# Decoding the gated product's weights through PSUM, and two banks instead of four for its first group

## The chip, the cores and the metric

The kernel runs on one core of a Trainium2 chip. Its engines are PE (matrix products, with PEld loading weights beside it), DVE (vector), ACT (scalar), POOL (GpSimd) and SP (which issues DMAs). Each has a queue of its own, worked off in order, and waits for the others by semaphores. The metric is the device time of one execution in microseconds, as a median of several runs.

## What is computed

Three layers in one program: an attention with pooled queries, a mixture of experts with a capacity, and a gated product. Only the last one is touched here:

```python
def _moe2_setup():
    n_tokens, d_model, d_ff = (1152, 512, 1536)
    ...
def _moe2_ref(x, w_a, w_b, w_out) -> np.ndarray:
    a = x @ w_a
    b = x @ w_b
    return (a * b @ w_out).astype(np.float32)
```

The three weights come as float64. The kernel turns each of their 64-bit words into a 32-bit one with integer operations (the decode), splits that into a high and a low part, and makes each product from three: high x high, low x high, high x low.

## The kernel before

**The gated product.** The 1536 inner columns are cut into 12 blocks f. For each f there are two upward products, s1(f, 0) with w_a and s1(f, 1) with w_b, and a downward one, s2(f) with w_out. Each is a unit of twelve matmuls on PE. The tokens go in groups: 512 wide, then 320 wide. PE's order is written out in `cons`: s1(0, 0), s1(0, 1), s1(1, 0), s1(1, 1), s2(0), s1(2, 0), s1(2, 1), s2(1), and so on, 36 units; unit k uses weight k. For f from 1 on, s1(f, 1) is unit 3f and s2(f) unit 3f + 4. Weights are decoded during the first group only; the second finds them ready.

**Around one f.** ACT copies s1(f, 0) out of PSUM (`copy_a`, L1428), DVE multiplies s1(f, 1) with that (`times`, L1431), ACT makes the high part gh (L1435), POOL the low part gl (L1438). s2(f) needs gh for its first eight matmuls and gl for its last four. There are two gh buffers and one gl.

**The decode.** Nine of the 36 words are ready when the first group starts. For each of the other 27, ACT writes the absolute value of the upper half into one of three SBUF ring buffers, parts of the tile y (`absval`, L1200); DVE makes four steps: step 0 (L1180) clamps it in place, step 1 (L1183) shifts and masks it in place, step 2 (L1186) adds the sign bit out of the upper half, step 3 (L1189) adds bits of the lower half and writes the word back where it was fetched. ACT then makes the word's high part (L1375), POOL its low part (L1378). `tick` puts the steps of two neighbouring words in turn on DVE's queue: step 0 of word k + 1, step 2 of k, step 1 of k + 1, step 3 of k.

**What sets the order.** `first` and `group` give each piece of work a due time on a made-up clock, sort by it and issue it so; the order on every engine is fixed by that, whatever the chip's times are. Slots for fetched words are released by `tick` and by the splits; the next fetch into a slot waits for them on SP's queue.

**PSUM.** Of the eight banks, four hold the sums of the downward product (`oa0` to `oa3`) and four, under the name `ab`, take the upward products in turn.

Of the kernel before, what the change touches and what calls it, by code (L numbers as in the profile page):

```python
# [9 lines left out]
F32 = mybir.dt.float32  # L10
# [305 lines left out]
def fused_kernel(tc, q, k, v, w_gate, w1, w2, cap_in, w_a, w_b, w_out, out):  # L316
    nc = tc.nc
# [15 lines left out]
    def as_f32(bits):  # L333
        return struct.unpack("<f", struct.pack("<I", bits))[0]

    def pool(name, **kw):
        return tc.tile_pool(name=name, bufs=1, **kw)
# [272 lines left out]
    def scatter(dst, idx, src, group):  # L610
        nc.gpsimd.memset(spacer, 0.0)
        inst = nc.gpsimd.indirect_dma_start(out=dst, out_offset=bass.IndirectOffsetOnAxis(ap=idx, axis=0),  # L612
                                            in_=src, in_offset=None)
        ins = inst.ins if hasattr(inst, "ins") else inst
        for o in groups.setdefault(group, []):
            tc.declare_no_dep(ins, o, reason="scattered rows are distinct")
        groups[group].append(ins)
# [214 lines left out]
    class Banks:  # L832
        n, wide = 0, None
# [335 lines left out]
    def halves(a):  # L1169
        return a.rearrange("p (h n) -> p h n", h=2)  # L1170

    def words(k):
        return halves(raw64[k].rearrange("p n w -> p (n w)")).rearrange("p h (n w) -> p h n w", w=2)

    def decode_step(hw, lw, c, step, out=None):
        ci = c.bitcast(I32)
        if step < 0:
            nc.vector.tensor_scalar(out=ci, in0=hw, scalar1=0x7FFFFFFF, scalar2=None, op0=ALU.bitwise_and)
        elif step == 0:
            nc.vector.tensor_scalar(out=c, in0=c, scalar1=as_f32(0x38000000), scalar2=as_f32(0x47EFFFFF),  # L1180
                                    op0=ALU.max, op1=ALU.min)
        elif step == 1:
            nc.vector.tensor_scalar(out=ci, in0=ci, scalar1=3, scalar2=0x3FFFFFF8,  # L1183
                                    op0=ALU.logical_shift_left, op1=ALU.bitwise_and)
        elif step == 2:
            nc.vector.scalar_tensor_tensor(out=ci, in0=hw, scalar=-0x40000000, in1=ci,  # L1186
                                           op0=ALU.bitwise_and, op1=ALU.bitwise_or)
        else:
            nc.vector.scalar_tensor_tensor(out=ci if out is None else out, in0=lw, scalar=29, in1=ci,  # L1189
                                           op0=ALU.logical_shift_right, op1=ALU.bitwise_or)  # L1190

    def decode_words(hw, lw, c):
        for step in range(-1, 4):
            decode_step(hw, lw, c, step)

    def decode(k, c, step, out=None):
        decode_step(words(k)[:, :, :, 1], words(k)[:, :, :, 0], c, step, out)

    def absval(k, c):
        nc.scalar.activation(c, words(k)[:, :, :, 1].bitcast(F32), AF.Abs)  # L1200
# [144 lines left out]
    pf = mid.enter_context(pool("psf", space=PSUM))  # L1345
# [9 lines left out]
    def wt(f, i, p, c=None):  # L1355
        t = (HI, LO)[p][cons.index((f, i))]
        return t if c is None else t[:, c * 128:c * 128 + 128]
# [10 lines left out]
            nc.vector.tensor_tensor(out=yl[:, c, 0:w], in0=src, in1=yh[:, c, 0:w].bitcast(F32), op=ALU.subtract)  # L1368

    ring = [y[:, 0:2, N:N + 256], y[:, 2:4, N:N + 256], y[:, 2:4, 0:256]]  # L1370

    def split_hi(k):
        if k >= KX:
            own(fp if k < KB else yp, k)
        nc.scalar.activation(halves(HI[k]), packed[k], AF.Copy)  # L1375
# [4 lines left out]
    def tick(k):  # L1380
        for d, i in ((1, 0), (0, 2), (1, 1), (0, 3)):
            if PK <= k + d < NK:
                n, at = k + d, k - 1 if k in SECOND else k
                out = words(at)[:, :, :, 1 if at < k else 0] if i == 3 else None
                decode(n, ring[n % 3], i, out)
                if i == 3:
                    packed[k] = out.bitcast(F32)
        if PK <= k + 2 < NK:
            absval(k + 2, ring[(k + 2) % 3])
# [5 lines left out]
    def first(plan):  # L1395
        DV, PO = T["dv"], T["po"]
        for k in range(PK - 2, NK):
            t = T["t0"] + (k - PK) * DV
            plan.append((t, lambda k=k: tick(k)))
            if ("t", k) in FREED:  # L1400
                plan.append((t, lambda k=FREED["t", k]: fetch(k)))
        ready = {}
        for k in range(NL, NK):
            t = PO * (k - NL) - T["p0"]
            if k >= PK:
                t = max(t, T["t0"] + (k - PK) * DV + .1)
            ready[k] = t + .5
            plan += [(t, lambda k=k: split_hi(k)), (t + .4, lambda k=k: split_lo(k))]
            if ("s", k) in FREED:
                plan.append((t + .5, lambda k=FREED["s", k]: fetch(k)))  # L1410
        return ready

    def group(o, w, nxt=None):
        by_token = o == 0
        oa = [pf.tile([128, 512], F32, name=f"oa{c}", bufs=1) for c in range(KD)]
        ab, gs = {}, {}
        asb, gg = y[:, 0, o:o + w], y[:, 1, o:o + w]

        def s1(f, i):
            p = ab[f, i] = pf.tile([128, 512], F32, name="ab", bufs=4)  # L1420
            seq = [(wt(f, i, 0, c), yh[:, c, 0:w]) for c in range(KD)]
            seq += [(wt(f, i, 1, c), yh[:, c, 0:w]) for c in range(KD)]
            seq += [(wt(f, i, 0, c), yl[:, c, 0:w]) for c in range(KD)]
            for n, (a, x) in enumerate(seq):
                nc.tensor.matmul(p[:, 0:w], a, x, start=(n == 0), stop=(n == len(seq) - 1))  # L1425
# [36 lines left out]
        for n, (f, i) in enumerate(cons):  # L1462
            now = max(now, ready.get(n, 0.0) + .05)
            if i == 2:
                now = max(now, t[f] + T["gl"] + .01)
                plan.append((now, lambda f=f: s2(f)))
            else:
                plan.append((now, lambda f=f, i=i: s1(f, i)))
                if i == 0:
                    plan.append((now + unit + .02, lambda f=f: copy_a(f)))  # L1470
                else:
                    t[f] = now + unit + .02
                    for d, fn in ((T["gg"], times), (T["gh"], g_hi), (T["gl"], g_lo)):
                        plan.append((t[f] + d, lambda f=f, fn=fn: fn(f)))
            now += unit
            if n == NK - 2 and nxt is not None:
                plan.append((now, lambda: split_y(nxt, min(W1, N - nxt))))
# [19 lines left out]
        def rows_out(t, last):  # L1497
            n = min(128, w - t)
            at = ids[min(o, W0)][:n, (o - min(o, W0) + t) // 128]
            rows = slots[RAW + t // 128][:n, 0:DM]  # L1500
            for g in range(0, KD, 2 if last else KD):
                cs = range(g, g + 2 if last else KD)
                p = pf.tile([128, 512], F32, name="ab", bufs=4)
                for c in cs:
                    nc.tensor.transpose(p[:n, (c - g) * 128:(c - g) * 128 + 128], ot[:, c, t:t + n], ident)
                r = rows[:, g * 128:(g + len(cs)) * 128]
                if last and g == 0:
                    nc.vector.tensor_scalar(out=r, in0=p[:n, 0:256], scalar1=at[:, 0:1], scalar2=None, op0=ALU.mult)
                else:
                    nc.scalar.activation(r, p[:n, 0:len(cs) * 128], AF.Copy, scale=at[:, 0:1])  # L1510
            scatter(out, at[:, 1:2].bitcast(I32), rows, "out")
        for t in range(0, w, 128):
            rows_out(t, nxt is None)
# [38 lines left out]
```

## Time and profile before

| | us |
|---|---|
| median of 3 runs (637.14 to 637.78) | 637.65 |
| the profiled execution | 637.94 |
| its span, first to last instruction | 636.2 |
| PE busy in the span | 575.6 (90%) |
| DVE busy | 392.9 (62%) |
| POOL busy | 364.6 (57%) |
| ACT busy | 307.4 (48%) |

The gated product takes the span's last 195 us: its first group runs from 441.5 to 559.8, the second one from there to about 624. The shares over the span mix stages with different limits, so the section with the rows reads single stretches. In a row of the timeline stand the start, the duration, the engine, the line, the operation, what it writes and reads, the shape, the count, and in brackets how long the engine stood idle before it and for whom. Instructions of one engine overlap by a little: the next may start before the duration of the last is over. Matmuls of a row marked x8 are eight in one.

### The profile page before, as it was taken

How to read it: one execution, taken by the hardware profiler on the slowest of the kernel's cores; microseconds unless marked ns; L12 is line 12 of the kernel's file. 1: busy time of each engine (PE TensorE's matmuls, PEld its weight loads, DVE VectorE, ACT ScalarE, POOL GpSimd, SP SyncE). 2: the span in 40 equal slices, each digit the busy share in tenths (PEclk: the TensorE clock that was granted, in tenths of full speed). 3: DMA queues.
4: the chain of work that ended last, by engine and by line, in shares of the span. 5: the costliest groups of instructions: out<-in, count | busy, mean ns of one | idle time of the engine just before them, and what ended most of it. 6: DMA issues, size and time to landing. Idle time of an engine off the chain costs nothing. (4 is left out here: it accounts for less than half of the span.)

```text
span 636.2 us, 10735 instructions
## 1 busy us (share of the span) xinstructions
PE 575.6 (90%) x3956; PEld 437.7 (69%) x3956; DVE 392.9 (62%) x702; ACT 307.4 (48%) x686; POOL 364.6 (57%) x291
## 2 busy tenths in 40 slices
PE   4798999999999999999997976998988798899993
PEld 3565666666666666656796974985776576699992
DVE  8667575756568595513568783746999999420001
ACT  6855566575656556455753422624344444321111
POOL 3966575757668896884538835751654565441112
PEclk9799999999999999999998888999999999999997
DMA  7902544224252624964397996999953020010001
GB/s 167 219 1 44 125 165 107 65 45 106 44 124 44 173 55 146 309 170 145 117 316 232 312 312 137 330 367 310 339 159 103 0 67 1 1 66 1 1 1 46
DMA packets 75998, 87.06 MB, mean 137 GB/s; under 512 B 24002, under 2 KB 57410, under 8 KB 75938
## 3 DMA queue, kind: packets, MB, share of 16 engines
q1 hardware_dynamic: 74258, 82.22, 44.8%
q0 software_dynamic: 1680, 4.07, 1.9%
q8 instruction: 33, 0.54, 0.3%
q14 instruction: 27, 0.22, 0.1%
HBM read 73.16 MB, written 6.43 MB: 125 GB/s over the span
## 5 line engine op out<-in xcount | busy, mean ns | idle before, releaser
L220 POOL TENSOR_TENSOR acc<-acc,E 128x1152 f32<-128x1152 f32 x52 | 137.5, 2644 | 52.3 <-ACT E L194 51.8
L161 DVE TENSOR_REDUCE MX<-tr 128x1 f32<-128x384 f32 x202 | 108.4, 554 | 74.8 <-PE tr L159 71.8
L194 ACT ACTIVATE E<-sc 128x288 f32<-128x288 f32 x288 | 108.1, 409 | 94.3 <-PE sc L193 89.7
L200 PE MATMUL pv<-E,vt 128*64 128x288 f32 x576 | 101.6, 431 | 0.0
L1425 PE MATMUL ab<-yh,w 128*128 128x512 f32 (+1 forms) x336 | 69.7, 349 | 0.0
L1425 PEld LDWEIGHTS ab<-yh,w 128*128 128x128 f32 x336 | 57.0, 188 | 6.8
L1438 POOL TENSOR_TENSOR gl<-y,gh 128x512 fp32r<-128x512 f32 (+1 forms) x24 | 27.9, 1164 | 54.3 <-PE oa L1455 47.2
L1378 POOL TENSOR_TENSOR w<-w,w 128x512 fp32r<-128x512 f32 x22 | 31.5, 1435 | 45.8 <-ACT w L1375 30.7
L1431 DVE TENSOR_TENSOR y<-ab,y 128x512 f32<-128x512 f32 (+1 forms) x24 | 14.1, 586 | 62.4 <-PE ab L1425 57.1
L200 PEld LDWEIGHTS pv<-E,vt 128*64 128x64 f32 x576 | 28.7, 134 | 26.0 <-issue 24.9
L1425 PE MATMUL ab<-yl,w 128*128 128x512 f32 (+1 forms) x168 | 38.2, 349 | 0.0
L220 POOL TENSOR_TENSOR acc<-E 128x1152 f32<-128x1152 f32 x8 | 21.2, 2651 | 29.3 <-ACT E L194 29.0
L192 PE MATMUL sc<-ra,even 128*128 128x288 f32 x108 | 34.8, 329 | 1.0 <-ACT E L194 1.0
L1375 ACT ACTIVATE w<-w 128x512 fp32r<-128x512 f32 x22 | 14.6, 675 | 38.4 <-DVE w L1189 38.4
L1425 PEld LDWEIGHTS ab<-yl,w 128*128 128x128 f32 x168 | 28.9, 188 | 3.3
L1183 DVE TENSOR_SCALAR y<-y 128x512 int32<-128x512 int32 x27 | 30.1, 1114 | 0.0
L192 PEld LDWEIGHTS sc<-ra,even 128*128 128x128 f32 x108 | 20.7, 192 | 13.0 <-ACT E L194 8.5
L1445 PE MATMUL oa<-w,gh 128*128 128x512 f32 x96 | 24.2, 394 | 4.3 <-ACT gh L1435 4.3
L159 PE MATMUL tr<-even,ra 128*128 128x384 f32 x74 | 27.1, 390 | 0.9 <-DVE MX L161 0.9
L1428 ACT ACTIVATE y<-ab 128x512 f32<-128x512 f32 (+1 forms) x24 | 12.2, 510 | 29.2 <-PE ab L1425 29.2
L1435 ACT ACTIVATE gh<-y 128x512 fp32r<-128x512 f32 (+1 forms) x24 | 13.2, 548 | 26.4 <-DVE y L1431 26.4
L1445 PEld LDWEIGHTS oa<-w,gh 128*128 128x128 f32 x96 | 17.7, 188 | 9.5 <-ACT gh L1435 6.0
(405 smaller groups left out, 1485.0 us busy)
## 6 DMA issues: line engine op xcount, KB each, us to landing
rw<-in_moe_w_dram SPq DMA_DIRECT2D x21, 512.0 KB, 9.9
s_even<-in_moe_w_dram SPq DMA_DIRECT2D x12, 512.0 KB, 9.7
s_ra<-in_moe_w_dram SPq DMA_DIRECT2D x12, 512.0 KB
w<-in_moe_w_dram SPq DMA_DIRECT2D x12, 512.0 KB, 9.0
vt<-in_v_dram SPq DMA_DIRECT2D x8, 576.0 KB
s_qs<-in_moe_w_dram SPq DMA_DIRECT2D x9, 512.0 KB, 7.8
w<-in_moe_w_a_dram SPq DMA_DIRECT2D x9, 512.0 KB, 9.4
qs<-in_q_dram SPq DMA_DIRECT2D x7, 576.0 KB
```

The source lines that it names most:

```text
L159: nc.tensor.matmul(tr[:, 0:384], s["t1"][:, o:o + 128], s["KH"][u][:, h, :], start=(x < 8 or h == 0), stop=(x < 8 or h == 1))
L161: nc.vector.tensor_reduce(out=MX[i % 2][:, x, u:u + 1], in_=tr[:, 0:384], axis=AX.X, op=ALU.max)
L192: nc.tensor.matmul(t[:, 0:HG], s["KH"][c // 3][:, h, cs], s["T1"][:, h, gs], start=True, stop=False)
L194: nc.scalar.activation(Es[c][:, h, gs], t[:, 0:HG], AF.Exp, scale=0.0625)
L200: nc.tensor.matmul(pvs[0][64 * h:64 * h + 64, g, 0:HG], s["vt"][:, h, c, :], Es[c][:, h, g * HG:g * HG + HG], start=(c == 0), stop=(c == N ...
L220: eng.tensor_tensor(out=acc, in0=acc if c > 1 else Es[0], in1=Es[c], op=ALU.add)
L1183: nc.vector.tensor_scalar(out=ci, in0=ci, scalar1=3, scalar2=0x3FFFFFF8, op0=ALU.logical_shift_left, op1=ALU.bitwise_and)
L1375: nc.scalar.activation(halves(HI[k]), packed[k], AF.Copy)
L1378: nc.gpsimd.tensor_tensor(out=halves(LO[k]), in0=packed[k], in1=halves(HI[k]).bitcast(F32), op=ALU.subtract)
L1425: nc.tensor.matmul(p[:, 0:w], a, x, start=(n == 0), stop=(n == len(seq) - 1))
L1438: nc.gpsimd.tensor_tensor(out=gs[f][1], in0=gg, in1=gs[f][0].bitcast(F32), op=ALU.subtract)
L1445: nc.tensor.matmul(oa[t // 128], gh[0][:, t:t + 128], wt(f, 2, p), start=(f == 0 and p == 0), stop=False)
```

## The change

Three things are changed, all in the gated product:

1. Two tiles of one PSUM bank each, `cb0` and `cb1`, take the intermediate word of the decode. Step 0 reads the SBUF ring and writes a bank; steps 1 and 2 read and write that bank; step 3 reads it and writes to SBUF as before. Neighbouring words use the two banks in turn.
2. In the first group the upward products go in turn through two banks (`ab`) instead of four.
3. In the second group, and for the transposed rows at its end, the turn is over `ab`, `cb0`, `ab`, `cb1`: four banks, as before.

```diff
-    def decode_step(hw, lw, c, step, out=None):
+    def decode_step(hw, lw, c, step, out=None, src=None):
...
-            nc.vector.tensor_scalar(out=c, in0=c, scalar1=as_f32(0x38000000), scalar2=as_f32(0x47EFFFFF),
+            nc.vector.tensor_scalar(out=c, in0=c if src is None else src, scalar1=as_f32(0x38000000), scalar2=as_f32(0x47EFFFFF),
                                     op0=ALU.max, op1=ALU.min)
...
     ring = [y[:, 0:2, N:N + 256], y[:, 2:4, N:N + 256], y[:, 2:4, 0:256]]
+    work = [halves(pf.tile([128, 512], F32, name=f"cb{i}", bufs=1)) for i in range(2)]
+    turn = [0]
+
+    def bank(wide):
+        if not wide:
+            return pf.tile([128, 512], F32, name="ab", bufs=2)
+        turn[0] += 1
+        name = ("ab", "cb0", "ab", "cb1")[turn[0] % 4]
+        return pf.tile([128, 512], F32, name=name, bufs=2 if name == "ab" else 1)
...
-                decode(n, ring[n % 3], i, out)
+                if i == 0:
+                    decode_step(None, None, work[n % 2], i, src=ring[n % 3])
+                else:
+                    decode(n, work[n % 2], i, out)
...
-            p = ab[f, i] = pf.tile([128, 512], F32, name="ab", bufs=4)
+            p = ab[f, i] = bank(not by_token)
...
-                p = pf.tile([128, 512], F32, name="ab", bufs=4)
+                p = bank(True)
```

The instructions stand in the same order on every engine; operands and waits differ. On DVE, words 19 and 20 of the decode with the L1431 of f = 4 between them (w_4965 and w_4966 are the fetched words, y holds the ring), before:

```order
L1180 TENSOR_SCALAR y<-y 128x2x256 [waits Activation_49]
L1186 SCALAR_TENSOR_TENSOR y<-w_4965,y 128x2x256 [waits DVE_49]
L1183 TENSOR_SCALAR y<-y 128x2x256 [waits DVE_49]
L1189 SCALAR_TENSOR_TENSOR w_4965<-w_4965,y 128x512 [waits DVE_49]
L1431 TENSOR_TENSOR y<-ab,y 128x512 [waits PE_49,Activation_49,Pool_49]
L1180 TENSOR_SCALAR y<-y 128x2x256 [waits Activation_49]
```

and now (cb_4975 and cb_4976 are the two banks; L1443 is the old L1431):

```order
L1180 TENSOR_SCALAR cb_4975<-y 128x512 [waits DVE_49,Activation_49]
L1186 SCALAR_TENSOR_TENSOR cb_4976<-w_4965,cb_4976 128x512
L1183 TENSOR_SCALAR cb_4975<-cb_4975 128x512 [waits DVE_49]
L1189 SCALAR_TENSOR_TENSOR w_4965<-w_4965,cb_4976 128x512 [waits DVE_49]
L1443 TENSOR_TENSOR y<-ab,y 128x512 [waits PE_49,Activation_49,Pool_49]
L1180 TENSOR_SCALAR cb_4976<-y 128x512 [waits DVE_49,Activation_49]
```

Nothing moved; L1180 waits for DVE's own earlier step as well, since it writes the bank which the L1189 ahead of it has read. On PE, two upward units of the first group (w_4960 and w_4961 are split weights), before:

```order
L1425 MATMUL ab<-yh,w_4960 128x512 x8
L1425 MATMUL ab<-yl,w_4960 128x512 x4
L1425 MATMUL ab<-yh,w_4961 128x512 [waits DVE_49]
L1425 MATMUL ab<-yh,w_4961 128x512 x7
L1425 MATMUL ab<-yl,w_4961 128x512 x4
```

and now:

```order
L1437 MATMUL ab<-yh,w_4960 128x512 [waits Activation_49]
L1437 MATMUL ab<-yh,w_4960 128x512 x7
L1437 MATMUL ab<-yl,w_4960 128x512 x4
L1437 MATMUL ab<-yh,w_4961 128x512 [waits DVE_49]
L1437 MATMUL ab<-yh,w_4961 128x512 x7
L1437 MATMUL ab<-yl,w_4961 128x512 x4
```

The order is the same. s1(f, 0) now waits for ACT's copy of s1(f - 1, 0), whose bank it takes; s1(f, 1) waited for DVE before too, now for the L1431 of f - 1, one f later than with four banks.

## Rows read from the trace of the kernel before

**Rows 1.** Stretches: PE, PEld, DVE, ACT, POOL busy us, granted clock, DMA.

```profile
core 0: us, PE busy (x) PEld busy (x) DVE busy (x) ACT busy (x) POOL busy (x), PEclk, DMA share, GB/s
...
470.00:545.00 75.00, 61.68 (x262) 48.12 (x261) 74.90 (x92) 32.24 (x55) 40.63 (x29) 1.00 0.17 53
...
560.00:624.00 64.00, 63.23 (x431) 62.96 (x430) 7.08 (x15) 11.84 (x27) 14.79 (x20) 1.00 0.05 17
```

**Rows 2.** Waits, 470 to 545 us: total us, times, longest.

```profile
PE oa L1448 <- POOL gl L1438: 9.8, 6, 2.2
```

**Rows 3.** Timeline of all engines, 487 to 501 us.

```profile
489.61 0.68 DVE L1431 TENSOR_TENSOR y<-ab,y 128x512 f32<-128x512 f32 x1
...
489.95 1.98 PE L1425 MATMUL ab<-yh,w 128*128 128x512 f32 x8
490.21 0.41 DVE L1180 TENSOR_SCALAR y<-y 128x512 f32<-128x512 f32 x1
...
490.47 1.33 POOL L1378 TENSOR_TENSOR w<-w,w 128x512 fp32r<-128x512 f32 x1 [1.68 <-ACT w L1375]
490.55 1.80 DVE L1186 SCALAR_TENSOR_TENSOR y<-w,y 128x512 int32<-128x512 int32 x1
...
492.61 0.68 DVE L1189 SCALAR_TENSOR_TENSOR w<-w,y 128x512 int32<-128x512 int32 x1
492.68 1.97 PE L1445 MATMUL oa<-w,gh 128*128 128x512 f32 x8
...
493.32 0.69 ACT L1375 ACTIVATE w<-w 128x512 fp32r<-128x512 f32 x1 [1.81 <-DVE w L1189]
...
494.08 1.30 POOL L1378 TENSOR_TENSOR w<-w,w 128x512 fp32r<-128x512 f32 x1 [2.28 <-ACT w L1375]
...
495.34 1.44 POOL L1438 TENSOR_TENSOR gl<-y,gh 128x512 fp32r<-128x512 f32 x1
...
496.84 1.19 PE L1448 MATMUL oa<-w,gl 128*128 128x512 f32 x4 [2.19 <-POOL gl L1438]
...
500.26 0.68 DVE L1431 TENSOR_TENSOR y<-ab,y 128x512 f32<-128x512 f32 x1
```

**Rows 4.** Single lines, 450 to 542 us: count, ns min/median/max, first and last start.

```profile
L1180 DVE TENSOR_SCALAR y<-y x26: 408/414/929, 450.0 to 540.5; 128x512 f32<-128x512 f32 x26
...
L1183 DVE TENSOR_SCALAR y<-y x26: 411/1522/1547, 452.6 to 541.5; 128x512 int32<-128x512 int32 x26
...
L1186 DVE SCALAR_TENSOR_TENSOR y<-w,y x18: 676/679/1818, 458.5 to 540.9; 128x512 int32<-128x512 int32 x18
...
L1189 DVE SCALAR_TENSOR_TENSOR w<-w,y x17: 678/680/1799, 460.6 to 535.3; 128x512 int32<-128x512 int32 x17
```

**Rows 5.** Single lines again: DVE lines that read PSUM, and POOL's L220.

```profile
L1431 DVE TENSOR_TENSOR y<-ab,y x10: 676/678/682, 449.4 to 539.9; 128x512 f32<-128x512 f32 x10
...
L161 DVE TENSOR_REDUCE MX<-tr x202: 512/557/560, 13.0 to 275.1; 128x1 f32<-128x384 f32 x101
...
L220 POOL TENSOR_TENSOR acc<-acc,E x52: 2628/2645/2659, 41.2 to 305.5; 128x1152 f32<-128x1152 f32 x52
...
L1487 DVE TENSOR_SCALAR s_ra<-oa,ids x2: 741/745/749, 559.3 to 559.9; 128x512 f32<-128x512 f32 x2
```

**Rows 6.** Timeline of DVE, 372 to 378 us, where each step waits for the last.

```profile
375.22 0.69 DVE L1186 SCALAR_TENSOR_TENSOR dc<-raw,dc 128x512 int32<-128x512 int32 x1
375.94 0.69 DVE L1189 SCALAR_TENSOR_TENSOR w<-raw,dc 128x512 int32<-128x512 int32 x1
```

**Rows 7.** Timeline of all engines, 440 to 460 us.

```profile
448.50 1.98 PE L1425 MATMUL ab<-yh,hl 128*128 128x512 f32 x8
...
450.03 0.93 DVE L1180 TENSOR_SCALAR y<-y 128x512 f32<-128x512 f32 x1
```

**Rows 8.** Timeline of PE, 440 to 565 us.

```profile
529.65 1.98 PE L1425 MATMUL ab<-yh,w 128*128 128x512 f32 x8
...
556.64 1.98 PE L1445 MATMUL oa<-w,gh 128*128 128x512 f32 x8
...
559.78 1.34 PE L1425 MATMUL ab<-yh,hl 128*128 128x320 f32 x8
```

## The prediction

> **What bounds the kernel now.** I read the stretches first. From 470 to 545 us DVE is busy 74.90 of 75 us and PE 61.68; from 560 to 624 us PE is busy 63.23 of 64 at a granted clock of 1.00 [rows 1]. So in the first group of the gated product DVE sets the pace, and PE in the second. The waits say how that reaches PE: in the same 75 us it stood 9.8 us, six times, before the low half of a downward product, waiting for gl from POOL [rows 2].
>
> The timeline of one f (f = 4) shows the chain [rows 3]. The product L1431 starts at 489.61, the next one at 500.26, so a round takes 10.65 us. PE needs less: a unit of twelve matmuls takes 492.68 - 489.95 = 2.73 (2.72 as the mean over the rounds), three of them 8.16. After L1431 come four decode steps, the last (L1189) at 492.61; ACT splits that word at 493.32, POOL does its low half at 494.08 and then gl at 495.34, and PE goes on at 496.84 after 2.19 idle. From that L1189's start to PE it is 4.23 us. Everything in it hangs on DVE's position.
>
> Why is DVE so slow? In the round it runs twelve decode steps and one L1431. In their fast form the rows are 408 and 411 ns for the two single-input steps and about 677 for the two double-input ones, but the medians or maxima of L1183, L1186 and L1189 are 1522, 1818 and 1799 [rows 4]. Start to start, the fast ones are 0.34 (490.21 to 490.55) and 0.60 (489.61 to 490.21) [rows 3]: three words of 2 x 0.34 + 2 x 0.60 = 1.88, and 0.60, make 6.24. The other 10.65 - 6.24 = 4.41 us are four steps that each start beside a POOL subtraction and take 1.1 longer: L1186 at 490.55 took 1.80 against the POOL row at 490.47 [rows 3]; POOL has four subtractions a round, three of them in these rows.
>
> **Part 1, the four steps.** Now every step has at most one SBUF operand among its inputs. The trace of before has no DVE instruction that writes PSUM, but many that read it. L1431 reads one PSUM and one SBUF tile: 676/678/682 over ten, never stretched. The 202 reductions L161 from PSUM stay within 512 to 560 although POOL ran 2.6 us additions L220 through that stage [rows 5]. I conclude that DVE work with one SBUF input at most doesn't meet POOL, so the 4.41 go. The price: the two single-input steps lose their fast form (0.34 to 0.60 each, taking L1431's spacing as the nearest row; 512 words in the same 678). A new wait comes in: step 0 of a word now writes the bank that the step right in front of it has just read, so DVE has to finish that one. A step that waits for the one ahead of it starts 375.94 - 375.22 = 0.72 after it instead of 0.60 [rows 6]. Sum per word d = 0.72 + 3 x 0.60 = 2.52; per round 3 x 2.52 + 0.60 = 8.16 (the step behind L1431 doesn't wait, so a little less), against PE's 8.16. DVE and PE are matched, and DVE starts with a lead.
>
> Bounds on d: below, nothing in the trace is quicker than 0.60 for 512 words with a PSUM operand, so four of them, 2.40. Above, the slowest full-width row with a PSUM input is L1487, 745 ns [rows 5]; start to start that is some 0.08 less, as with L1431 (0.68 and 0.60): 4 x 0.665 + 0.12 = 2.78. I take 2.52, since L1431 has the same kind of operands. [...]
>
> **Part 2, how late DVE may be.** Number PE's units by the weight they use: unit 2 starts at 448.50 [rows 7], and unbroken PE starts unit u at 448.50 + 2.72 (u - 2). On DVE, decoding resumes behind the first L1431 at 450.03 [rows 7]; between the first and the ninth L1431 (f = 8) lie 23 words and then 8 x 0.60. Two demands are the tightest:
> - Two banks. s1(f + 1, 1), unit 3f + 3, now waits until L1431 of f has read the bank. For f = 8 that is unit 27, due at 516.50. L1431 is done at 450.03 + 23 d + 4.80 + 0.08 = 454.91 + 23 d, at d = 2.52 at 512.87: 3.6 us to spare; it fits up to d = 2.68.
> - The chain to gl for f up to 5, where POOL has one more word's low half ahead of it: 450.03 + 14 d + 2.40 + 0.60 + (d - 0.72) + 4.23 = 456.54 + 15 d, against unit 19's low half (two thirds into it), 448.50 + 17 x 2.72 + 1.81 = 496.55. At d = 2.52 2.2 us to spare; it fits up to d = 2.67.
> When PE sets the pace, L1431 runs right behind unit 3f, and the same chain of 0.2 + 0.6 + 1.8 + 4.23 = 6.8 us has three units and 1.81 = 9.97. What queues behind a late L1431 is decode of later words, some seven units ahead of PE. POOL was busy 40.63 and ACT 32.24 of the 75 us [rows 1], 5.8 and 4.6 us a round, and are not next. The fetches are released by the decode steps and move forward with them.
>
> The first downward unit (unit 4, f = 0) has the same chain: 450.03 + 1.80 + 4.23 = 456.06, against 448.50 + 2 x 2.72 + 1.81 = 455.75. The two steps ahead of that L1431 lose their stretch, so it comes some 0.5 sooner; I count unit 4 unbroken.
>
> **Part 3, the rest at nothing.** Step 0 frees the SBUF ring earlier for ACT, which nobody waits for. In the second group the products turn through four banks as before, ab, cb0, ab, cb1; its DVE and POOL work is unchanged. What covers this is PE itself, busy 63.23 of 64 [rows 1].
>
> **The sum.** Unit 35 starts at 448.50 + 33 x 2.72 = 538.26. It took 559.78 - 556.64 = 3.14 before, because gl has one buffer, and will again [rows 8]: the second group starts at 541.40 instead of 559.78, 18.4 us sooner. Span 636.2 - 18.4 = 617.8, and with the 1.74 around it 619.6 for the profiled execution of 637.94. That execution lies 0.29 above the median of 637.65, so 619.3 for the median.
>
> **Rivals.** *DVE still the bound, by a smaller margin.* If a PSUM operand costs a step what it costs L1487, d = 2.78, unit 27 starts at 454.91 + 63.94 = 518.85, 2.35 late: 621.6. Every further 0.1 in d costs 2.3 us. For it: no DVE write to PSUM is in the trace, and the two demands have only 0.15 of room in d. Against: L1431. [...]
> *Slower: reading and writing one bank.* Steps 1 and 2 read a bank and write the same bank. If that took two passes, 1.20 start to start, d = 0.72 + 0.60 + 2.40 = 3.72. Unit 27 started at 529.65 before [rows 8]; 454.91 + 23 d reaches that at d = 3.25, from where the change loses. At 3.72 it is 23 x 0.47 = 10.8 late: 648.5. Nothing in the trace speaks for it; no row excludes it.
> *The change doesn't do what it says.* If POOL still stretched the steps by 4.41 a round, 1.47 a word, d = 3.99 and 17.0 late: 654.7. The 202 steady L161 rows speak against it.
> *PE slows down when it is dense.* Against: 1.00 in 560 to 624 us [rows 1].
>
> **How the numbers follow.** PE unbroken, 618.5 to 620.5: 0.72. DVE still somewhat ahead of PE as the bound, 620.5 to 626.5: 0.13; heavily, up to 636: 0.06. Within 0.2% of before (what a measurement of this kernel can tell from no change): 0.02. Slower: 0.07, of which the bank is 0.05. Hence faster 0.91, same 0.02, slower 0.07. The lower end, 618.3, is the sum without the 0.4 that the last unit waits and with 0.6 for the spread of the runs (637.14 to 637.78); the upper end, 626.5, takes in d up to 2.99. That leaves out some 0.13 above and little below.
>
> **What would show it.** L1180 and L1183 each about 0.68 and no decode step above 0.75; a round of 8.2 us between neighbouring L1431; DVE idle before L1431 for PE; PE busy nearly all of 470 to 540 us; the first 320-wide matmul near 541.4. Wrong if L1183 or L1186 lasts over 0.9, if long steps remain beside POOL's subtractions, or if PE waits for L1431 before every s1(f, 1), which would mean that two banks are too few.

## The result, and the profile after

The changed kernel took 620.0 us (median of four runs, 619.41 to 620.85) beside 637.39 for the kernel before on the same chip: a ratio of 0.9735, 95% interval 0.9709 to 0.976. On a second chip, beside a further experiment, it was 0.9691 (0.9652 to 0.9729). The profiled execution took 619.41 with a span of 617.6, 18.6 us less than the 636.2 of before. Lines behind 1370 moved: L1431 is now L1443, L1425 is L1437, L1375 and L1378 are L1384 and L1387, L1448 is L1460.

First the stretches, read as [rows 1]:

```profile
core 0: us, PE busy (x) PEld busy (x) DVE busy (x) ACT busy (x) POOL busy (x), PEclk, DMA share, GB/s
...
470.00:540.00 70.00, 69.89 (x309) 57.55 (x308) 54.35 (x91) 33.27 (x57) 38.60 (x31) 1.00 0.14 44
```

PE is busy 69.89 of 70 us where it was busy 61.68 of 75, and its granted clock stays at 1.00. No wait of PE for gl is left in the list of waits (9.8 us in [rows 2]); DVE now waits for PE:

```profile
DVE y L1443 <- PE ab L1437: 13.6, 4, 7.5
```

None of these four waits lies in the rounds in which three words each are decoded. One of 0.79 us comes before the first product, the other three after the ninth, from here on:

```profile
518.82 0.69 DVE L1443 TENSOR_TENSOR y<-ab,y 128x512 f32<-128x512 f32 x1 [1.56 <-PE ab L1437]
```

From 455 to 517 us neither engine waits for the other: each works without a pause, at 8.15 and 8.16 us a round.

PE's timeline gives the length of the first group, from its first matmul to the first one of width 320 (columns as in [rows 8]):

```profile
440.85 2.51 PE L1437 MATMUL ab<-yh,hl 128*128 128x512 f32 x8 [1.23 <-DVE yh L1363]
...
447.80 1.98 PE L1437 MATMUL ab<-yh,hl 128*128 128x512 f32 x8
...
515.80 1.98 PE L1437 MATMUL ab<-yh,w 128*128 128x512 f32 x8
...
537.56 1.98 PE L1457 MATMUL oa<-w,gh 128*128 128x512 f32 x8
...
540.70 1.34 PE L1437 MATMUL cb<-yh,hl 128*128 128x320 f32 x8
```

Unit 2 starts at 447.80 and unit 27 at 515.80: 25 units in 68.00 us, 2.72 each, with no gap. The group lasts 540.70 - 440.85 = 99.85 us. Before, the 320-wide matmul was at 559.78 [rows 8], and the first one, in the same timeline of PE before, here:

```profile
441.51 2.51 PE L1425 MATMUL ab<-yh,hl 128*128 128x512 f32 x8 [1.22 <-DVE yh L1363]
```

That made 118.27 us. The 18.4 between them are the gain but for 0.2: the span is 18.6 shorter.

Now the decode steps, line by line, as in [rows 4] (count, ns min/median/max, first and last start):

```profile
L1180 DVE TENSOR_SCALAR cb<-y x27: 682/694/696, 445.9 to 519.4; 128x512 f32<-128x512 f32 x27
...
L1183 DVE TENSOR_SCALAR cb<-cb x27: 689/693/699, 446.6 to 520.6; 128x512 int32<-128x512 int32 x27
...
L1186 DVE SCALAR_TENSOR_TENSOR cb<-w,cb x18: 681/684/687, 455.8 to 520.0; 128x512 int32<-128x512 int32 x18
...
L1189 DVE SCALAR_TENSOR_TENSOR w<-w,cb x18: 675/678/681, 456.9 to 521.2; 128x512 int32<-128x512 int32 x18
```

Nothing is stretched any more: 699 is the largest value, where 929 to 1818 stood [rows 4]. The fast form of the single-input steps (408 and 411) is gone as well, at 694 and 693. One round on DVE's timeline:

```profile
462.71 0.69 DVE L1443 TENSOR_TENSOR y<-ab,y 128x512 f32<-128x512 f32 x1
463.31 0.68 DVE L1180 TENSOR_SCALAR cb<-y 128x512 f32<-128x512 f32 x1
463.90 0.69 DVE L1186 SCALAR_TENSOR_TENSOR cb<-w,cb 128x512 int32<-128x512 int32 x1
464.50 0.69 DVE L1183 TENSOR_SCALAR cb<-cb 128x512 int32<-128x512 int32 x1
465.10 0.68 DVE L1189 SCALAR_TENSOR_TENSOR w<-w,cb 128x512 int32<-128x512 int32 x1
465.88 0.69 DVE L1180 TENSOR_SCALAR cb<-y 128x512 f32<-128x512 f32 x1
...
470.86 0.69 DVE L1443 TENSOR_TENSOR y<-ab,y 128x512 f32<-128x512 f32 x1
...
511.62 0.69 DVE L1443 TENSOR_TENSOR y<-ab,y 128x512 f32<-128x512 f32 x1
```

Start to start the steps are 0.60 apart (463.31 to 463.90, 463.90 to 464.50), except where step 0 waits for the step right in front of it: 465.10 to 465.88, 0.78. A round is 470.86 - 462.71 = 8.15 us, down from 10.65.

### The profile page after: what moved, and what is told of

Read it like the earlier page. It is cut to its first block, busy times and chain, and to the rows that moved or that the text cites. A ratio compares the mean times of both kernels' runs of the same rounds, so it can differ in the third digit from the quotient of the medians.

```text
span 617.6 us, 10757 instructions
## 1 busy us (share of the span) xinstructions
PE 571.5 (93%) x3956; PEld 438.4 (71%) x3956; DVE 366.4 (59%) x702; ACT 307.7 (50%) x686; POOL 358.7 (58%) x291
## 5 line engine op out<-in xcount | busy, mean ns | idle before, releaser
L220 POOL TENSOR_TENSOR acc<-acc,E 128x1152 f32<-128x1152 f32 x52 | 137.4, 2643 | 52.8 <-ACT E L194 52.3
L1450 POOL TENSOR_TENSOR gl<-y,gh 128x512 fp32r<-128x512 f32 (+1 forms) x24 | 26.5, 1104 | 57.3 <-PE oa L1467 47.2
L1437 PE MATMUL ab<-yh,w 128*128 128x512 f32 (+1 forms) x256 | 56.2, 362 | 0.0
L1443 DVE TENSOR_TENSOR y<-ab,y 128x512 f32<-128x512 f32 (+1 forms) x24 | 14.2, 590 | 68.2 <-PE ab L1437 64.5
L1387 POOL TENSOR_TENSOR w<-w,w 128x512 fp32r<-128x512 f32 x22 | 29.5, 1347 | 35.2 <-ACT w L1384 19.9
L1437 PEld LDWEIGHTS ab<-yh,w 128*128 128x128 f32 x256 | 44.9, 188 | 6.6
L220 POOL TENSOR_TENSOR acc<-E 128x1152 f32<-128x1152 f32 x8 | 21.2, 2651 | 28.8 <-ACT E L194 28.4
L1437 PE MATMUL ab<-yl,w 128*128 128x512 f32 (+1 forms) x128 | 30.7, 362 | 0.0
L1384 ACT ACTIVATE w<-w 128x512 fp32r<-128x512 f32 x22 | 14.4, 667 | 23.4 <-DVE w L1189 23.3
L1437 PEld LDWEIGHTS ab<-yl,w 128*128 128x128 f32 x128 | 22.7, 188 | 3.3
L192 PE MATMUL sc<-tb,KH 128*128 128x288 f32 x72 | 23.9, 341 | 0.4 <-ACT E L194 0.4
L192 PE MATMUL sc<-ra,KH 128*128 128x288 f32 x72 | 23.4, 332 | 0.8 <-ACT E L194 0.8
L159 PE MATMUL tr<-KH,tb 128*128 128x384 f32 x60 | 21.8, 383 | 2.0 <-DVE MX L161 2.0
```

The costliest lines, as they stand in the source:

```text
L159: nc.tensor.matmul(tr[:, 0:384], s["t1"][:, o:o + 128], s["KH"][u][:, h, :], start=(x < 8 or h == 0), stop=(x < 8 or h == 1))
L192: nc.tensor.matmul(t[:, 0:HG], s["KH"][c // 3][:, h, cs], s["T1"][:, h, gs], start=True, stop=False)
L220: eng.tensor_tensor(out=acc, in0=acc if c > 1 else Es[0], in1=Es[c], op=ALU.add)
L1387: nc.gpsimd.tensor_tensor(out=halves(LO[k]), in0=packed[k], in1=halves(HI[k]).bitcast(F32), op=ALU.subtract)
L1443: nc.vector.tensor_tensor(out=gg, in0=ab[f, 1][:, 0:w], in1=asb, op=ALU.mult)
L1450: nc.gpsimd.tensor_tensor(out=gs[f][1], in0=gg, in1=gs[f][0].bitcast(F32), op=ALU.subtract)
```

## The experiments

The theory is the prediction's: DVE sets the pace in the first group because POOL's subtractions hold its decode steps; steps with one SBUF input at most are out of that; PE then runs unbroken. Rivals were that the steps are slow for another reason, that two banks cost PE time, and that DVE, not PE, is still the bound (8.15 against 8.16 us a round can't tell). The first four experiments ran on one chip (before: 633.84 there), the last three on another (637.55), so ratios and the length of the first group are compared, not bare times. In the second, third and fifth experiment the first eight matmuls of the group took 3.58, 3.66 and 3.92 us instead of 2.51; the profile gives a granted clock of 7, 8 and 8 tenths in the fortieth of the span in which they lie, against 9 or more in the changed kernel, and unit 2 comes 0.2 to 0.6 us later behind the first matmul. Where small differences count, the length is taken from unit 2 on: 540.70 - 447.80 = 92.90 in the changed kernel.

**Two banks alone.** The kernel before, its decode untouched, with parts 2 and 3 of the change (the function `bank` and its two uses; one of them here):

```diff
-            p = ab[f, i] = pf.tile([128, 512], F32, name="ab", bufs=4)
+            p = ab[f, i] = bank(not by_token)
```

> The kernel before with the two banks alone: the upward products of the first group turn through two banks, the decode stays in SBUF. Theory: DVE sets the pace here, and the bank comes free only some 0.4 us after PE wants it (the product at 500.26 lasts to 500.94, the next s1(f, 1) started at 500.60); PE stands 2.19 us for gl later in the same round, which takes that up. So 637 to 638, a round of 10.65 us between neighbouring products L1431. Rival, two banks cost PE by themselves: 0.4 in each of eight rounds or more, 640 to 641.

Measured: ratio 1.0027 (0.9993 to 1.0061), the first group 559.16 - 440.96 = 118.20 us against 118.27, a round 499.70 - 489.06 = 10.64. PE's waits in 441 to 560 us (lines stand nine behind those of the kernel before):

```profile
PE oa L1457 <- POOL gl L1447: 5.6, 5, 1.4
...
PE ab L1434 <- DVE y L1440: 2.4, 2, 2.2
PE ab L1434 <- ACT y L1437: 2.2, 4, 0.6
```

PE now does wait for the banks, 4.6 us in all, and about that much less for gl: 5.6 us, where the kernel before has 10.4 in the same stretch. With DVE setting the pace, the two banks only moved PE's idle time. They are no part of the gain either; they make room for the other two. The rival's 640 would be a ratio of 1.004 and isn't excluded by the interval; the length of the group excludes it.

**POOL writes and doesn't read.** The kernel before, with POOL's subtractions in the first group, and those for gl in the second too, replaced by fills of the same tiles (lines as in the kernel before):

```diff
-        nc.gpsimd.tensor_tensor(out=halves(LO[k]), in0=packed[k], in1=halves(HI[k]).bitcast(F32), op=ALU.subtract)
+        nc.gpsimd.memset(halves(LO[k]).bitcast(F32), 0.0)
...
-            nc.gpsimd.tensor_tensor(out=gs[f][1], in0=gg, in1=gs[f][0].bitcast(F32), op=ALU.subtract)
+            nc.gpsimd.memset(gs[f][1].bitcast(F32), 0.0)
```

> The kernel before, but POOL's subtractions in the first group and those for gl in both are replaced by a fill with zeros of the same tiles: POOL writes as much SBUF as before and reads none. Left out are the low parts of 33 decoded weights and of the gated product. Theory: the decode steps with two SBUF inputs are stretched because POOL reads SBUF at the same time; without that L1186 and L1189 stay at 0.68, the round falls from 10.65 to PE's 8.16, and the time to 619 to 621. The steps with one input may still be stretched, if the fast form also collides with POOL's writes; then a round is longer by up to the length of POOL's fills. Rival, the steps are slow for another reason (their operands, DMA traffic, PE): rows as before and 637.

Measured: ratio 0.971 (0.9677 to 0.9742), the first group 541.34 - 441.41 = 99.93 us:

```profile
441.41 3.58 PE L1425 MATMUL ab<-yh,hl 128*128 128x512 f32 x8 [1.43 <-DVE yh L1363]
...
541.34 1.33 PE L1425 MATMUL ab<-yh,hl 128*128 128x320 f32 x8
```

The decode is the old one in SBUF, and the rows are:

```profile
L1180 DVE TENSOR_SCALAR y<-y x27: 415/422/745, 446.3 to 520.5; 128x512 f32<-128x512 f32 x27
...
L1183 DVE TENSOR_SCALAR y<-y x27: 412/424/703, 446.7 to 521.4; 128x512 int32<-128x512 int32 x27
...
L1186 DVE SCALAR_TENSOR_TENSOR y<-w,y x18: 673/687/691, 455.5 to 520.8; 128x512 int32<-128x512 int32 x18
...
L1189 DVE SCALAR_TENSOR_TENSOR w<-w,y x18: 674/683/693, 456.5 to 521.7; 128x512 int32<-128x512 int32 x18
```

This shows the cause: with POOL's reads gone the two-input steps (L1186, L1189) stay under 0.70 us, and the same gain comes without any PSUM. The single-input steps in their fast form still stretch a little, by up to 0.33. The timeline of all engines shows both beside a fill; the first row is of an earlier round:

```profile
470.89 0.69 DVE L1431 TENSOR_TENSOR y<-ab,y 128x512 f32<-128x512 f32 x1 [1.30 <-PE ab L1425]
...
489.95 0.64 POOL L1438 MEMSET gl<- 128x512 f32 x1 [5.85 <-PE oa L1448]
490.03 0.69 DVE L1186 SCALAR_TENSOR_TENSOR y<-w,y 128x512 int32<-128x512 int32 x1
...
490.52 1.27 POOL L1378 MEMSET w<- 128x512 f32 x2
490.63 0.70 DVE L1183 TENSOR_SCALAR y<-y 128x512 int32<-128x512 int32 x1
```

L1186 at 490.03 starts inside the fill and runs at its 0.69; L1183 at 490.63 takes 0.70 instead of 0.42. The fills are also shorter than the subtractions (0.52 against 1.3 us). Whether the stretch of L1180 and L1183 is small for that reason is not separated here; that L1186 isn't stretched at all beside a fill doesn't hang on it. The shorter fills bring gl forward too, but that alone could not have shortened DVE's round, which was busy 74.90 of 75 us; now DVE stands 1.30 us in a round for PE (470.89).

**Step 0 in SBUF.** The changed kernel, with step 0 in place in the ring, and step 1 going from the ring to the bank:

```diff
-                    decode_step(None, None, work[n % 2], i, src=ring[n % 3])
+                    decode(n, ring[n % 3], i)
+                elif i == 1:
+                    nc.vector.tensor_scalar(out=work[n % 2].bitcast(I32), in0=ring[n % 3].bitcast(I32), scalar1=3,
+                                            scalar2=0x3FFFFFF8, op0=ALU.logical_shift_left, op1=ALU.bitwise_and)
```

> The changed kernel, but step 0 works in place in the SBUF ring as before, and step 1 is the one that reads SBUF and writes the bank. Theory: only step 0, in its fast form, can still meet POOL, so its rows spread from 0.41 to about 1.5; step 1, one SBUF input, stays at 0.69, steps 2 and 3 at 0.68. DVE has less to do than in the changed kernel, yet PE is the bound there, so the time stays at 619.5 to 621. Rival, DVE still sets the pace in the changed kernel (its rounds of 8.15 and PE's of 8.16 can't be told apart in the trace): then up to 0.26 us a word less, some 5 us, 615.

Measured: ratio 0.9718 (0.969 to 0.9746), the first group 536.75 - 436.52 = 100.23 us, from unit 2 (443.71) on 93.04 against 92.90. L1397 is step 1, L1446 the product.

```profile
L1180 DVE TENSOR_SCALAR y<-y x26: 412/418/1337, 444.6 to 515.5; 128x512 f32<-128x512 f32 x26
...
L1397 DVE TENSOR_SCALAR cb<-y x26: 679/683/691, 446.3 to 516.4; 128x512 int32<-128x512 int32 x26
```

```profile
482.24 0.69 DVE L1446 TENSOR_TENSOR y<-ab,y 128x512 f32<-128x512 f32 x1 [1.10 <-PE ab L1440]
```

Step 0 is the only one that is still stretched (412 to 1337 ns); step 1, a single-input step too, takes 679 to 691 ns with its output in PSUM, where it took 411 at the least in SBUF [rows 4], and isn't. And DVE now waits for PE within the rounds (1.10 us at 482.24): 16.7 us in seven waits in the first group, against 13.6 in four in that of the changed kernel, none of which lay in the rounds. DVE has less to do and nothing is won: PE is the bound in the changed kernel. The rival, 615 as a gain of 5 us, falls on the first group's length and on the ratio (615 of 637.39 would be 0.965, below the interval). The bare 615.79 lies outside the 619.5 to 621 that was expected and seems to bear the rival out, but it belongs to a chip where the kernel before takes 633.84.

**Step 0 twice.** The changed kernel with one more full-width DVE step for each word:

```diff
-                    decode_step(None, None, work[n % 2], i, src=ring[n % 3])
+                    for _ in range(2):
+                        decode_step(None, None, work[n % 2], i, src=ring[n % 3])
```

> The changed kernel with step 0 of each word done twice (the result is the same): about 0.60 to 0.79 us more DVE work for each word. Theory: the ninth product (f = 8) was done at 512.31 and PE wanted its bank for unit 27 at 515.80, 3.5 us of room; 23 words lie ahead of it, 23 x 0.6 = 13.8 to 23 x 0.75 = 17.3 us, so unit 27 comes 10.3 to 13.8 late: 630 to 634. PE then waits before s1(f, 1) for the product, or before the low half for gl. Rival, DVE has time to spare (busy 54 of 70 us in 470 to 540): under 622.

Measured: 629.55, ratio 0.9935 (0.9913 to 0.9957), the first group 552.19 - 438.05 = 114.14 us, 14.3 more than in the changed kernel. The time is just under the expected 630 to 634, which were reckoned for the first chip; the ratio times 637.39 is 633.2. From DVE's timeline (L1444 is the product):

```profile
483.47 0.69 DVE L1444 TENSOR_TENSOR y<-ab,y 128x512 f32<-128x512 f32 x1
...
493.81 0.69 DVE L1444 TENSOR_TENSOR y<-ab,y 128x512 f32<-128x512 f32 x1
```

and from PE's:

```profile
500.99 1.20 PE L1461 MATMUL oa<-w,gl 128*128 128x512 f32 x4 [1.58 <-POOL gl L1451]
...
525.57 3.10 PE L1438 MATMUL ab<-yh,w 128*128 128x512 f32 x8 [1.89 <-DVE y L1444]
...
530.01 1.99 PE L1458 MATMUL oa<-w,gh 128*128 128x512 f32 x8
```

A round takes 10.34, that is (10.34 - 8.15) / 3 = 0.73 more a word. PE waits in the two places that the prediction named: for gl, and before unit 27 (525.57) for its bank. Unit 27 stands 525.57 - 438.05 = 87.52 us behind the first matmul instead of 515.80 - 440.85 = 74.95: 12.6 late, and 23 x 0.73 less the 3.5 of room is 13.3. The other 1.7 of the 14.3 lies in unit 27 itself, which takes 530.01 - 525.57 = 4.44 instead of 2.72, without a wait. Its first eight matmuls took 3.10 us and its last four 1.71, where a unit of the changed kernel takes 1.98 and 1.07, and the profile gives a granted clock of 8 tenths for 518.5 to 534.2 and of 9 or more behind that. Two earlier units were as long, 4.45 and 4.44 us: their first eight matmuls took 3.35 at 481.48, behind a wait of 1.56 for gl (480.30), and 3.56 at 502.23, behind the wait at 500.99; the clock was 8 tenths for 471.4 to 487.1 and for 502.8 to 518.5. Why it fell stays open: in the kernel before, waits of up to 2.2 us [rows 2] left it at 1.00 [rows 1]. So DVE's idle time after 522 us was no spare: the room is about 3.5 us by the ninth product.

**Step 3 with two SBUF inputs.** The changed kernel, with step 2 writing the SBUF ring:

```diff
...
+                elif i == 2:
+                    nc.vector.scalar_tensor_tensor(out=ring[n % 3].bitcast(I32), in0=words(n)[:, :, :, 1],
+                                                   scalar=-0x40000000, in1=work[n % 2].bitcast(I32),
+                                                   op0=ALU.bitwise_and, op1=ALU.bitwise_or)
                 else:
-                    decode(n, work[n % 2], i, out)
+                    decode(n, ring[n % 3], i, out)
```

> The changed kernel, but step 2 writes its word into the SBUF ring, so that step 3 has two SBUF inputs as before; steps 0, 1 and 2 keep a PSUM operand. Theory: only step 3 is stretched, where it starts beside a POOL subtraction (rows from 0.68 to 1.8), the others stay at 0.68 to 0.70. The wait of step 0 for the step ahead of it goes (0.72 to 0.60), which gives 0.36 a round back; with one to three stretched steps of 0.3 to 1.1 us a round, a round is 8.2 to 9.5 and the time 620 to 630. Rival, any step is stretched or none is: all rows spread, or the time is below 620.

Measured: 622.29, ratio 0.9754 (0.9708 to 0.9799), the first group 542.79 - 440.55 = 102.24 us, 2.4 more than in the changed kernel. Of these 0.6 lie ahead of unit 2, where PE's first eight matmuls took 3.92 us instead of 2.51; from unit 2 (448.07) on it is 94.72 against 92.90, 1.8 more. L1399 is step 2.

```profile
L1183 DVE TENSOR_SCALAR cb<-cb x27: 683/686/699, 446.3 to 525.4; 128x512 int32<-128x512 int32 x27
L1189 DVE SCALAR_TENSOR_TENSOR w<-w,y x18: 675/932/1658, 457.7 to 526.0; 128x512 int32<-128x512 int32 x18
...
L1399 DVE SCALAR_TENSOR_TENSOR y<-w,cb x18: 670/672/679, 456.5 to 524.8; 128x512 int32<-128x512 int32 x18
```

Only the step with two SBUF inputs spreads. Its DVE row and the POOL row beside it, from the two engines' timelines:

```profile
479.93 1.27 DVE L1189 SCALAR_TENSOR_TENSOR w<-w,y 128x512 int32<-128x512 int32 x1
```

```profile
479.34 1.31 POOL L1387 TENSOR_TENSOR w<-w,w 128x512 fp32r<-128x512 f32 x1
```

POOL ends at 480.65, DVE at 481.20, 0.55 later; for L1186 at 490.55 and its POOL row in [rows 3] it is 0.55 too. That looks as if the step does nothing until POOL is through and then needs little under its usual time (0.55 against 0.68); the profile shows no wait for it, only the longer row. PE meets it before unit 27, where it waits 0.74 us for the product; that unit starts 517.67 - 448.07 = 69.60 us behind unit 2 instead of 68.00. The wait of step 0 for the step ahead of it is gone, as expected: 0.60 (L1189 at 474.90, L1180 at 475.50). The total can't be told from the changed kernel's on that chip (intervals 0.9708 to 0.9799 and 0.9652 to 0.9729 overlap); the first group's length and the rows are what tells them apart.

**The changed kernel again, and a try at what is left.** In the first unit PE stands 0.67 us for the last of the four low parts of y (yl), before the last yl matmul:

```profile
444.72 0.50 PE L1437 MATMUL ab<-yl,hl 128*128 128x512 f32 x1 [0.67 <-DVE yl L1368]
```

The try puts the yl matmuls of the first two units behind both units' yh matmuls:

```diff
...
-                plan.append((now, lambda f=f, i=i: s1(f, i)))
+                if by_token and f == 0:
+                    plan.append((0.0 if i == 0 else 0.001, lambda i=i: s1(0, i, 0)))
+                    plan.append((now if i else now + 0.002, lambda i=i: s1(0, i, 1)))
+                else:
+                    plan.append((now, lambda f=f, i=i: s1(f, i)))
```

(s1(f, i, 0) issues the eight matmuls with yh, s1(f, i, 1) the four with yl.)

> The changed kernel again, to stand beside the next one on the same chip: 619.5 to 621.

> The changed kernel, with the first two units of the first group taken apart: the eight matmuls with yh of s1(0, 0), those of s1(0, 1), then the four with yl of each. PE stood 0.67 us for the last yl and started again with a longer matmul; both should go, 0.7 to 0.9 us, 619 to 620 against the changed kernel beside it. Rival, what waits next (gh and gl of f = 0, which need both units) takes it back: no difference.

Measured, six runs each: 618.98 and 618.26, ratios 0.9691 (0.9652 to 0.9729) and 0.9698 (0.966 to 0.9736): no difference that these runs can tell (the medians lie 0.7 apart one way, the ratios 0.0007 the other). In the profile the first group is 0.92 us shorter: 541.96 - 442.11 = 99.85 for the changed kernel again, 98.93 for the try:

```profile
439.00 4.31 PE L1438 MATMUL ab<-yh,hl 128*128 128x512 f32 x16 [1.23 <-DVE yh L1363]
...
537.93 1.33 PE L1438 MATMUL cb<-yh,hl 128*128 128x320 f32 x8
```

The wait for yl is gone and what follows keeps it so. That is 0.15% of the time, under the spread of the runs here.

## Why the prediction was right

**What bounds the kernel, and why.** Right: DVE set the pace and POOL's reads were the reason. The prediction had it from four stretched steps beside four subtractions; the fills in place of subtractions showed that it is the reads.

**The price of a step.** d = 2.52 was right as the mean of a round: three words in 8.15 - 0.60 = 7.55. Two terms were off against each other, and that they cancel is luck. The wait of step 0 costs 0.18 (0.78 start to start), not 0.12; but it falls only in two of a round's three words, as the bracket behind the sum said: 2 x 0.18 = 3 x 0.12. Writing PSUM, for which the trace of before had no row, cost what reading it did but for 6 to 16 ns: 694 and 684 for the lines that write it, 678 for L1189, which only reads it, all 0.60 apart. The upper bound of 2.78 doesn't show: with a PSUM operand L1186 takes 684 against 679 without [rows 4], and the spacing is the same 0.60.

**How late DVE may be.** Right. The ninth product was to be done at 512.87, or 512.17 on the clock of this run, where unit 2 starts 0.70 earlier (447.80 against 448.50); it ended at 511.62 + 0.69 = 512.31. That it fits to 0.14 is partly luck, since two things that the sum left out nearly cancel. Decoding resumed 448.68 - 447.80 = 0.88 us behind the start of unit 2 and not 1.53 (450.03 - 448.50), because the two steps ahead of the first product lost their stretch; the prediction mentions that but doesn't count it. And the second product waited 0.82 us for POOL:

```profile
448.68 0.69 DVE L1180 TENSOR_SCALAR cb<-y 128x512 f32<-128x512 f32 x1
...
454.55 0.69 DVE L1443 TENSOR_TENSOR y<-ab,y 128x512 f32<-128x512 f32 x1 [0.82 <-POOL gl L1450]
```

Unit 27 was to start at 516.50, so 515.80, and did. The doubled step 0 tested the slope: 12.6 us late for 13.3. One sign did not come: in the rounds DVE doesn't stand before the product for PE, it keeps pace with it. That PE is the bound there is shown by the experiment with step 0 in SBUF and not by a wait in the changed kernel.

**The sum.** The second group was to start 18.4 us sooner. From the first matmul on it is 118.27 - 99.85 = 18.4. Unit 4 was unbroken, and the last unit took 540.70 - 537.56 = 3.14 again. The profiled execution, forecast at 619.6, took 619.41. The median of 620.0 stands 0.7 above the forecast 619.3; the four runs differ by 1.4, so that needs no cause.

**Rivals.** DVE as a smaller bound: the experiment with step 0 in SBUF takes DVE work away and the first group doesn't shorten. Two passes for a bank that is read and written: L1183 does both at 693 ns, 0.60 start to start, so it falls. POOL still in the way: no step above 699. A slower PE: clock 1.00 at 69.89 of 70.

## What to carry to other kernels

Where DVE and POOL both work on SBUF, compare the minimum and the maximum of each DVE line: here L1183, L1186 and L1189 had maxima 1.1 us above their minima, beside POOL subtractions of 1.3. That only raises the suspicion; replacing POOL's reads by fills is what showed it. Giving each DVE step one SBUF input at most, by keeping the intermediate in PSUM, cost the fast form here (0.34 to 0.60 us for 512 words) and a wait, together 8.15 - 6.24 = 1.9 us a round, and won because the stretches cost more, 4.4 us a round. Before giving banks away for that, work out when each of the fewer banks has to be free; here the room was 3.5 us, and one more step a word used it up.

## What the runs showed of the hardware that I had not expected

A DVE step that waits for the DVE step right in front of it starts 0.78 us after that one's start where it writes the PSUM bank that the one in front has read (465.10 to 465.88), against 0.72 with SBUF alone [rows 6] and 0.60 without the wait. A POOL fill of 0.64 us (489.95) didn't hold a DVE step with two SBUF inputs (0.69 at 490.03), but two fills of 1.27 together (490.52) did hold one of the fast single-input form (0.70 at 490.63 instead of 0.42). And PE lost more than the length of a wait: with step 0 doubled, the unit behind a wait of 1.89 us took 4.44 us instead of 2.72, where the profile gives a granted clock of 8 tenths (518.5 to 534.2).
